# Stage 2 of three batches in other product shapes, four low parts on GpSimd, and another slot for the state rows' operand

## The chip, the cores and the metric

The kernel runs on one core of a Trainium2 chip. The metric is the device time of one execution in microseconds; lower is better. The engines named below are PE (TensorE: the matrix products), PEld (its weight loads), DVE (VectorE), ACT (ScalarE), POOL (GpSimd) and SP (the queue that issues most DMAs).

## The reference

There are B = 8 batches, H = 8 heads, S = 512 tokens, 32 state rows and D = 64 values per head. Cut to what matters:

```
scores  = x @ state^T / 8;  a  = softmax(scores)      # tokens look at the state
xread   = a @ state
scores2 = state @ x^T / 8;  a2 = softmax(scores2)     # state rows look at the tokens
sread   = a2 @ x
y   = concat([xread, sread], rows)                     # 544 rows a batch, 8 * 64 = 512 wide
out = ((y @ w1) * (y @ w2)) @ w3 @ w_out               # 512 -> 1024 -> 1024 -> 512
```

The weights arrive as float64, x and state as float32; the output is float32.

## The kernel before

**Products at full precision from float32r parts.** A float32 operand is split into a high part (ACT casts it to float32r, L96) and a low part (DVE subtracts the high part, L97). A product is three float32r products: high by low, high by high, low by high. On PE one such product loads 128 x 128 stationary values (LDWEIGHTS) and lets a moved operand of 512 columns stream through.

**Weights.** `w3 @ w_out` is formed once at the start and kept split as `wo_hi` and `wo_lo` (1024 rows in 8 blocks `ft` of 128, 512 columns). For each batch, state times w1 and w2 gives small matrices `sw_hi`, `sw_lo` (L260 to L282), so that stage 1 can go from the attention weights straight to the hidden layer.

**The stages of a batch b.**

- `stage1(b, ft)`, for ft = 0 to 7: 12 products (L306) into one buffer of two PSUM banks (pool `ps_2`, three buffers in rotation, `two_banks()`), one bank for w1, one for w2. Then `hidden`: ACT copies one half (L290), DVE multiplies it with the other (L291), and `split` makes `g_hi` (ACT, L96) and `g_lo` (DVE, L97), [128 hidden values x 512 tokens] each.
- `stage2(gs, tt)`, for tt = 0 to 3: 24 products (`project`, L316; stationary is a 128-token slice of `g_hi` or `g_lo`, moved are 512 columns of `wo_hi` or `wo_lo`) into one bank (pool `ps_o`, two buffers, `bank()`). ACT copies the bank to a `tmp` tile (L329, `store`), and a DMA writes it out.
- After tt = 0, the side steps for batch b + 1 follow in PE's order: two units of `sw` (into `ps_2`), the scores of both softmaxes (into `ps_2`, L146 in the function `per_head`, moved operand `x_d`), the read of the state rows of batch b (into `ps_o`, L242), and two more units of `sw` (into `ps_2`). The softmax work on DVE and ACT then runs beside tt = 1 to 3. The scores are read from PSUM by a DVE transpose (L186), a DVE maximum (L189) and two ACT exponentials (L196).

PE's and SP's orders are those in which the code is written; a buffer of a pool in rotation is free again when its last reader has ended. Batch 0 is handled apart, mixed with the loading and conversion of the weights. `FORMS` in the change speaks of batches 4, 5 and 6.

**State rows.** After batch 7, `state_rows` takes the 256 gathered rows `sread` through the same layers. Its moved operand `grp_sr` holds high and low part side by side; for each of 64 steps a product of 512 columns (L507) and one of 256 columns (L508) alternate, each with its own weights. Its stage 2 is two more calls of `stage2`.

Of the kernel before, what the change touches and what calls it, by code (L numbers as in the profile page):

```python
# [22 lines left out]
F32 = mybir.dt.float32  # L23
F32R = mybir.dt.float32r
# [3 lines left out]
ALU = mybir.AluOpType  # L28
AX = mybir.AxisListType
P = 128  # L30
# [3 lines left out]
LAST = 5  # L34
PARTS = {0: (640, 1024), 1: (512, 1024)}
WARM = 15

@with_exitstack
def attn_bilinear_kernel(
# [10 lines left out]
    nc = tc.nc  # L50
    B, _, NT, H, D = x_s.shape
    S = NT * P
    NP = H // 2
    NS = st.shape[3]
    KT = H * NS // P
    FT, DO = w34_k.shape[0], out.shape[2]
# [9 lines left out]
    att = ctx.enter_context(tc.tile_pool(name="att", bufs=2))  # L66
# [7 lines left out]
    unused = ps_o.tile([P, NF], F32, name="ps_o")  # L74
    for n in range(WARM):
        nc.tensor.matmul(unused[:, :P], zeros, zeros, start=True, stop=True)
# [7 lines left out]
    wo = {part: const.tile([P, FT, DO], F32R, name=f"wo_{part}") for part in ("hi", "lo")}  # L84
    const.tile([P, 32], F32, name="pad_1")

    def bank():
        return ps_o.tile([P, NF], F32, name="ps_o")

    def two_banks():  # L90
        return ps_2.tile([P, 2, NF], F32, name="ps_2")

    def split(hi, lo, src):

        return (
            nc.scalar.copy(out=hi, in_=src),  # L96
            nc.vector.tensor_tensor(out=lo, in0=src, in1=hi.bitcast(F32), op=ALU.subtract),  # L97
        )


# [49 lines left out]
    def load_x(b):  # L150
        sts[b] = att.tile([P, NP, NS], F32, name="st")
        nc.sync.dma_start(out=sts[b], in_=st[b])
        x_tiles[b] = att.tile([P, NP, S], F32, name="x_d", bufs=1)
        nc.sync.dma_start(out=x_tiles[b], in_=x_d[b])

    def load_tokens(b):
        token_tiles[b] = att.tile([P, NT, H, D], F32, name="x_s", bufs=1)
        nc.sync.dma_start(out=token_tiles[b], in_=x_s[b])
# [15 lines left out]
    def attention_steps(b):  # L174
# [3 lines left out]
        def scores():  # L178
# [41 lines left out]
            nc.vector.transpose(out=flat(at), in_=flat(s1))  # L220
            at_tiles[b] = [att.tile([P, KT, S], F32R, name=f"at_{part}", bufs=1) for part in ("hi", "lo")]
            last = split(*at_tiles[b], at)
            yield

# [38 lines left out]
    def sw_steps(b):  # L263
        sw_tiles.setdefault(b, {})

        def unit(half, i):
            ps = two_banks()
            as_q = ps.rearrange("p k (c f) -> p k c f", c=2)
            per_head(as_q, b, lambda rows, j: w_sb[rows, 2 * half:2 * half + 2, i, j])
            sw_tiles[b][half, i] = sw_pair()  # L270
            split(*sw_tiles[b][half, i], ps)

        return [(lambda half=half, i=i: unit(half, i)) for half in range(HALF) for i in range(2)]

    def sw_quarter(b, quarter, i):
        tiles = sw_tiles.setdefault(b, {})
        half, c = divmod(quarter, 2)
        if c == 0:
            tiles[half, i] = sw_pair()
        ps = two_banks()[:, :, :NQ]  # L280
        per_head(ps, b, lambda rows, j: w_sb[rows, quarter, i, j])
        split(*(t[:, :, c * NQ:(c + 1) * NQ] for t in tiles[half, i]), ps)  # L282


    last_split, stored = [], []

    def hidden(ps, n, g_hi, g_lo):
        a_sb = main.tile([P, NF], F32, name="tmp", bufs=4)
        with tc.high_priority():
            nc.scalar.copy(out=a_sb[:, :n], in_=ps[:, 0, :n])  # L290
            nc.vector.tensor_tensor(out=a_sb[:, :n], in0=a_sb[:, :n], in1=ps[:, 1, :n], op=ALU.mult)  # L291
            last_split[:] = split(g_hi, g_lo, a_sb[:, :n])

    def new_g():
        return [main.tile([P, NF], F32R, name=f"g_{part}", bufs=FT) for part in ("hi", "lo")]

    def stage1(b, ft, gs):
        half, c = divmod(ft * P, NF)
        ps = two_banks()
        hi, lo = at_tiles[b]  # L300
        for i in range(2):
            w_hi, w_lo = sw_tiles[b][half, i]
            k = 0
            for kt in range(KT):
                for w, a in ((w_hi, lo), (w_hi, hi), (w_lo, hi)):
                    nc.tensor.matmul(  # L306
                        ps[:, i], w[:, kt, c:c + P], a[:, kt], start=(k == 0), stop=(k == 3 * KT - 1)
                    )
                    k += 1
        gs.append(new_g())  # L310
        hidden(ps, S, *gs[-1])

    def project(ps, gs, tt, ft):
        g_hi, g_lo = (g[:, tt * P:(tt + 1) * P] for g in gs[ft])
        for k, (g, w) in enumerate(((g_hi, "lo"), (g_hi, "hi"), (g_lo, "hi"))):
            nc.tensor.matmul(  # L316
                ps[:, :DO], g, wo[w][:, ft, :], start=(ft == 0 and k == 0), stop=(ft == FT - 1 and k == 2)
            )

    def stage2(gs, tt, dests):  # L320
        ps = bank()
        for ft in range(FT):
            project(ps, gs, tt, ft)
        store(ps, dests)

    def store(ps, dests):
        o = main.tile([P, NF], F32, name="tmp", bufs=4)[:, :DO]
        with tc.high_priority():
            stored[:] = [nc.scalar.copy(out=o, in_=ps[:, :DO])]  # L329
        for (dest, first, n), queue in zip(dests, cycle((nc.scalar, nc.sync))):  # L330
            queue.dma_start(out=dest, in_=o[first:first + n])

# [2 lines left out]
    def side_steps(b):  # L335


        if b == B:
            return [[reads[b - 1]], [], [], []]
        scores, reads[b], a2 = attention_steps(b)  # L340
        w = sw_steps(b)
        softmax = scores()
        first = partial(islice, softmax, 3)
        if b == 1:
            def rest():

                with tc.issue_after(stored[0].ins):
                    yield from softmax

            return [[first], [reads[0], w[0], w[1]], [], [rest], [w[2], w[3]], []]  # L350

        product = partial(islice, softmax, 1)
        return [[w[0], w[1], product, reads[b - 1], w[2], w[3], lambda: softmax], [], [], []]

    def run(steps):
        for step in steps:
            for _ in step() or ():
                pass

    def batch_stage2(b, gs):  # L360
        side = side_steps(b + 1)
        for tt in range(NT):
            stage2(gs, tt, [(out[b, tt * P:(tt + 1) * P], 0, P)])
            run(side[tt])
        if b + 1 < B:
            load_tokens(b + 1)
        if b + 2 < B:
            load_x(b + 2)


    with tc.tile_pool(name="pro", bufs=2) as pro:
# [43 lines left out]
        gs, acc, early = [], [], range(2)  # L415
# [64 lines left out]
        for tt in range(NT):  # L480
            dests = [(out[0, tt * P:(tt + 1) * P], 0, P)]
# [7 lines left out]
    late = ctx.enter_context(tc.tile_pool(name="late", bufs=1))  # L489


    def state_rows():
        n = B * NS

        sr = late.tile([P, NP, 2, n], F32R, name="grp_sr")
        split(sr[:, :, 1], sr[:, :, 0], sread)
        gs = []
        for ft in range(FT):
            quarter, c = divmod(ft * P, NQ)
            ps = two_banks()  # L500
            for i in range(2):
                wh, wl = (late.tile([P, NP * P], F32R, name=f"grp_z{q}", bufs=3) for q in range(2))
                as_w = lambda t: t.rearrange("p (j f) -> p j f", j=NP)
                split(as_w(wh), as_w(wl), w_sb[:, quarter, i, :, c:c + P])
                for kt in range(NP):
                    ks = slice(kt * P, (kt + 1) * P)
                    nc.tensor.matmul(ps[:, i], wh[:, ks], sr[:, kt], start=(kt == 0), stop=False)  # L507
                    nc.tensor.matmul(ps[:, i, :n], wl[:, ks], sr[:, kt, 1], start=False, stop=(kt == NP - 1))  # L508
            gs.append([g[:, :n] for g in new_g()])
            sums = main.tile([P, 2, n], F32, name="tmp", bufs=4)  # L510
            halves = ps.rearrange("p i (half n) -> p i half n", n=n)
            nc.scalar.copy(out=sums, in_=halves[:, :, 1])
            nc.vector.tensor_tensor(out=sums, in0=sums, in1=halves[:, :, 0], op=ALU.add)
            nc.vector.tensor_tensor(out=sums[:, 0], in0=sums[:, 0], in1=sums[:, 1], op=ALU.mult)
            split(*gs[-1], sums[:, 0])
        for tt in range(n // P):
            stage2(gs, tt, [(out[tt * PER + q, S:], q * NS, NS) for q in range(PER)])


    for b in range(1, B):  # L520
        gs = []
        for ft in range(FT):
            stage1(b, ft, gs)
        batch_stage2(b, gs)
    with tc.issue_after(last_split[0].ins), tc.issue_after(last_split[1].ins):
        state_rows()
# [44 lines left out]
```

## Time and profile before

| | |
|---|---|
| timed executions | median 501.03 us (500.69 to 501.37, 2 runs) |
| profiled execution, first to last instruction (the span) | 498.4 us; some 2.6 us of the timed execution lie around it |
| PE busy | 492.3 us, 99% of the span, 3054 product records |
| DVE busy | 285.7 us, 57% |
| ACT busy | 219.3 us, 44% |
| POOL busy | 0.2 us, four small memsets |
| clock granted to PE | 0.999 of full speed over the span |

A product in the trace overlaps the next, since products are pipelined: its own duration (0.39 us for 512 columns) is longer than the distance from its start to the start of the next. What a product costs is that distance. A "timeline" row gives start and duration in us, engine, line, operation and tiles; a row of "groups" gives busy us and mean ns, then idle time ahead.

### The profile page before, as it was taken

To read this page: it belongs to the slowest core of one execution; us is meant where nothing else is said; L and a number is where in the kernel's file an instruction comes from. 1 tells how busy PE (TensorE), PEld (TensorE's weight loads), DVE (VectorE), ACT (ScalarE), POOL (GpSimd) and SP (SyncE) were. 2 spreads that over 40 slices of the span, in tenths; PEclk is the share of its full clock that TensorE was granted. 3 is DMA by queue.
4 is the path that set the end of the run, shared out by engine and by line. 5 is a ranking of instruction groups with operands and counts; after the bars stand their busy time and mean duration, and the time that the engine had idled before them with its cause. 6 is when DMAs were issued, how large, how long until landed. Compare 5 with 4: busy or idle time off the path is not lost.

```text
span 498.4 us, 7562 instructions
## 1 busy us (share of the span) xinstructions
PE 492.3 (99%) x3054; PEld 362.8 (73%) x3054; DVE 285.7 (57%) x394; ACT 219.3 (44%) x325; POOL 0.2 (0%) x4
## 2 busy tenths in 40 slices
PE   8999999999999999999999999999999999999996
PEld 6444467767867886788678867886788678888885
DVE  5669896772539343934393539354934493530780
ACT  4777884443444244334333434243424342431650
POOL 0000000000000000000000000000000000000000
PEclk9999999999999999999999999999999999999999
DMA  8996962013400350035003500350035003301001
GB/s 343 364 380 237 364 264 33 11 47 80 181 22 19 79 189 23 20 79 188 21 27 76 185 22 27 77 184 22 26 78 183 22 26 78 93 24 49 21 1 42
DMA packets 52323, 52.41 MB, mean 105 GB/s; under 512 B 42304, under 2 KB 43328, under 8 KB 47680
## 3 DMA queue, kind: packets, MB, share of 16 engines
q1 hardware_dynamic: 47488, 43.27, 26.3%
q10 hardware_dynamic: 4800, 8.65, 4.6%
q8 instruction: 24, 0.39, 0.3%
q14 instruction: 11, 0.09, 0.1%
HBM read 38.27 MB, written 8.91 MB: 95 GB/s over the span
## 4 chain that ended last, share of the span: by engine, by line
PE 95%; DVE 2%; ACT 2%; DMA 1%; issue 0%; DVEq 0%
PE ps_o L316 38%; PE ps L306 35%; PE ps L146 7%; PE ps L507 3%; PE ps_o L402 3%; PE ps_o L389 3%; PE ps L389 3%; PE ps L508 2%; PE ps_o L242 1%; DMA raw<-in_w_k_dram 1%; ACT ulps L125 0%; ACT w_sb L117 0%; ACT wo_hi L96 0%; DVE w L133 0%; DVE work L204 0%; DVE wo_lo L97 0%
## 5 line engine op out<-in xcount | busy, mean ns | idle before, releaser
L316 PE MATMUL ps_o<-wo_lo,g_hi 128*128 128x512 f32 x272 | 107.0, 394 | 0.0
L316 PE MATMUL ps_o<-wo_hi,g_hi 128*128 128x512 f32 x272 | 106.0, 390 | 0.0
L316 PE MATMUL ps_o<-wo_hi,g_lo 128*128 128x512 f32 x272 | 105.9, 389 | 0.0
L306 PE MATMUL ps<-at_lo,sw_hi 128*128 128x512 f32 x256 | 100.1, 391 | 0.0
L306 PE MATMUL ps<-at_hi,sw_lo 128*128 128x512 f32 x256 | 99.6, 389 | 0.0
L306 PE MATMUL ps<-at_hi,sw_hi 128*128 128x512 f32 x256 | 99.6, 389 | 0.0
L291 DVE TENSOR_TENSOR tmp<-tmp,ps 128x512 f32<-128x512 f32 x64 | 43.9, 687 | 77.0 <-ACT tmp L290 76.9
L97 DVE TENSOR_TENSOR g_lo<-tmp,g_hi 128x512 fp32r<-128x512 f32 (+1 forms) x72 | 47.5, 661 | 41.7 <-ACT g_hi L96 41.6
L96 ACT CAST g_hi<-tmp 128x512 fp32r<-128x512 f32 (+1 forms) x72 | 43.1, 599 | 53.6 <-DVE tmp L291 48.8
L290 ACT COPY tmp<-ps 128x512 f32<-128x512 f32 x64 | 37.7, 589 | 62.8 <-PE ps L306 52.2
L316 PEld LDWEIGHTS ps_o<-wo_lo,g_hi 128*128 128x128 f32 x272 | 51.0, 188 | 18.0 <-issue 7.5
L316 PEld LDWEIGHTS ps_o<-wo_hi,g_lo 128*128 128x128 f32 x272 | 51.1, 188 | 10.8
L316 PEld LDWEIGHTS ps_o<-wo_hi,g_hi 128*128 128x128 f32 x272 | 51.1, 188 | 10.3
L97 DVE TENSOR_TENSOR sw_lo<-ps,sw_hi 128x1024 fp32r<-128x1024 f32 (+1 forms) x34 | 38.4, 1155 | 32.8 <-ACT sw_hi L96 32.8
L306 PEld LDWEIGHTS ps<-at_lo,sw_hi 128*128 128x128 f32 x256 | 48.1, 188 | 10.9 <-issue 1.1
L306 PEld LDWEIGHTS ps<-at_hi,sw_hi 128*128 128x128 f32 x256 | 48.1, 188 | 10.2 <-issue 0.2
L306 PEld LDWEIGHTS ps<-at_hi,sw_lo 128*128 128x128 f32 x256 | 48.1, 188 | 10.0
L329 ACT COPY tmp<-ps_o 128x512 f32<-128x512 f32 x34 | 19.8, 583 | 76.1 <-PE ps_o L316 76.1
L96 ACT CAST sw_hi<-ps 128x1024 fp32r<-128x1024 f32 (+1 forms) x34 | 31.7, 967 | 14.3 <-PE ps L146 14.2
L146 PE MATMUL ps<-w_sb,st 64*32 64x512 f32 (+1 forms) x544 | 31.6, 572 | 0.0
L402 PE MATMUL ps_o<-w_sb,w 128*128 128x512 f32 x64 | 28.5, 599 | 0.1
L402 PEld LDWEIGHTS ps_o<-w_sb,w 128*128 128x128 f32 x64 | 11.8, 190 | 15.9 <-issue 13.8
(65 smaller groups left out, 417.9 us busy)
## 6 DMA issues: line engine op xcount, KB each, us to landing
raw<-in_w_k_dram SPq DMA_DIRECT2D x8, 1024.0 KB, 6.6
x_d<-in_x_d_dram SPq DMA_DIRECT2D x8, 1024.0 KB, 7.1
raw<-in_w_dram SPq DMA_DIRECT2D x8, 1024.0 KB, 6.3
x_s<-in_x_s_dram SPq DMA_DIRECT2D x8, 1024.0 KB, 5.4
out_dram<-tmp ACTq DMA_DIRECT2D x32, 256.0 KB, 2.0
raw<-in_w3t_dram SPq DMA_DIRECT2D x4, 1024.0 KB, 7.2
a_t<-work SPq DMA_DIRECT2D x96, 32.0 KB, 1.9
sread<-turned SPq DMA_DIRECT2D x128, 4.0 KB, 1.7
```

What stands on the lines that cost most here:

```text
L96: nc.scalar.copy(out=hi, in_=src),
L97: nc.vector.tensor_tensor(out=lo, in0=src, in1=hi.bitcast(F32), op=ALU.subtract),
L146: nc.tensor.matmul(ps[j * NS:(j + 1) * NS, q], sts[b][rows, j], moving(rows, j), start=True, stop=True)
L290: nc.scalar.copy(out=a_sb[:, :n], in_=ps[:, 0, :n])
L291: nc.vector.tensor_tensor(out=a_sb[:, :n], in0=a_sb[:, :n], in1=ps[:, 1, :n], op=ALU.mult)
L306: nc.tensor.matmul(ps[:, i], w[:, kt, c:c + P], a[:, kt], start=(k == 0), stop=(k == 3 * KT - 1))
L316: nc.tensor.matmul(ps[:, :DO], g, wo[w][:, ft, :], start=(ft == 0 and k == 0), stop=(ft == FT - 1 and k == 2))
L329: stored[:] = [nc.scalar.copy(out=o, in_=ps[:, :DO])]
L389: nc.tensor.matmul(w34_ps[i][:, :DO], chunks[k][:, DO + i * P:DO + (i + 1) * P], w_out[k], start=(k == 0), stop=(k == FT - 1),)
L402: nc.tensor.matmul(w34_ps[i][:, :DO], w3s[i][:, k * P:(k + 1) * P], w_out[k], start=(k == 0), stop=(k == FT - 1))
L507: nc.tensor.matmul(ps[:, i], wh[:, ks], sr[:, kt], start=(kt == 0), stop=False)
L508: nc.tensor.matmul(ps[:, i, :n], wl[:, ks], sr[:, kt, 1], start=False, stop=(kt == NP - 1))
```

## The change

- `FORMS = {4: 16, 5: "halves", 6: 4}`: in `batch_stage2`, tt = 1, 2 and 3 of these three batches take another form of stage 2; tt = 0 and the other batches keep theirs.
  - Batch 5, "halves": each product of 512 columns becomes two of 256 columns with the same stationary operand (48 products in place of 24 per tt). The two halves go to two banks of one `two_banks()` buffer of `ps_2`, not to a `ps_o` bank, and `store` copies each half by itself.
  - Batches 4 and 6, "runs": one product of 512 columns as before, but the moved row is read as 16 (batch 4) or 4 (batch 6) values of the first half, then as many of the second, in turn. PSUM then holds the columns in that order, written contiguously, and ACT's copy in `store` puts them back.
- In batch 3, `g_lo` of the odd ft (1, 3, 5, 7) is made on GpSimd in place of DVE.
- The state rows' `sr` lies in the slot of `x_s` (pool `att`) in place of a tile of its own in pool `late`; with that the `grp_z` tiles of `late` move to lower addresses.

The diff, cut to its core:

```
+FORMS = {4: 16, 5: "halves", 6: 4}
...
-    def split(hi, lo, src):
+    def split(hi, lo, src, rest=None):
         return (
             nc.scalar.copy(out=hi, in_=src),
-            nc.vector.tensor_tensor(out=lo, in0=src, in1=hi.bitcast(F32), op=ALU.subtract),
+            (rest or nc.vector).tensor_tensor(out=lo, in0=src, in1=hi.bitcast(F32), op=ALU.subtract),
         )
...
-        hidden(ps, S, *gs[-1])
+        hidden(ps, S, *gs[-1], nc.gpsimd if b == 3 and ft % 2 else None)
...
+    def project_halves(ps, gs, tt, ft):
+        g_hi, g_lo = (g[:, tt * P:(tt + 1) * P] for g in gs[ft])
+        for k, (g, w) in enumerate(((g_hi, "lo"), (g_hi, "hi"), (g_lo, "hi"))):
+            for half in range(2):
+                cols = slice(half * DO // 2, (half + 1) * DO // 2)
+                nc.tensor.matmul(
+                    ps[:, half, cols], g, wo[w][:, ft, cols],
+                    start=(ft == 0 and k == 0), stop=(ft == FT - 1 and k == 2),
+                )
+
+    def project_runs(ps, gs, tt, ft, run):
+        g_hi, g_lo = (g[:, tt * P:(tt + 1) * P] for g in gs[ft])
+        for k, (g, w) in enumerate(((g_hi, "lo"), (g_hi, "hi"), (g_lo, "hi"))):
+            nc.tensor.matmul(
+                ps[:, :DO], g, wo[w][:, ft, :].rearrange("p (h c e) -> p c h e", h=2, e=run),
+                start=(ft == 0 and k == 0), stop=(ft == FT - 1 and k == 2),
+            )
+
-    def stage2(gs, tt, dests):
+    def stage2(gs, tt, dests, form=None):
+        if form == "halves":
+            ps = two_banks()
+            for ft in range(FT):
+                project_halves(ps, gs, tt, ft)
+            store(ps, dests, [(slice(h * DO // 2, (h + 1) * DO // 2), ps[:, h, h * DO // 2:(h + 1) * DO // 2]) for h in range(2)])
+            return
         ps = bank()
...
+            if parts:
+                stored[:] = [nc.scalar.copy(out=o[:, cols], in_=src) for cols, src in parts]
+            elif run:
+                stored[:] = [nc.scalar.copy(
+                    out=o.rearrange("p (h c e) -> p c h e", h=2, e=run),
+                    in_=ps[:, :DO].rearrange("p (c h e) -> p c h e", h=2, e=run),
+                )]
...
-            stage2(gs, tt, [(out[b, tt * P:(tt + 1) * P], 0, P)])
+            stage2(gs, tt, [(out[b, tt * P:(tt + 1) * P], 0, P)], FORMS.get(b) if tt else None)
...
-        sr = late.tile([P, NP, 2, n], F32R, name="grp_sr")
+        sr = att.tile([P, NP, 2, n], F32R, name="x_s", bufs=1)
```

How instructions stand before on PE in batch 5, from the scores of batch 6 (the tile `ps_2_2887`) to the first products of tt = 1 (numbers tell buffers apart; `waits` names the semaphores of the engines or DMA queues that a row waits for):

```order
L146 MATMUL ps_2_2887<-x_d_2671,st_2669 32x512 [waits DMAHW3_49]
L146 MATMUL ps_2_2887<-x_d_2671,st_2669 32x512 x7
L242 MATMUL ps_o_2896<-x_s_2667,a2_t_2566 32x64 [waits DMAHW7_49,DMAHW1_49,DMAHW0_49]
L242 MATMUL ps_o_2896<-x_s_2667,a2_t_2566 32x64 [waits DMAHW6_49,DMAHW7_49,DMAHW5_49,DMAHW4_49]
L242 MATMUL ps_o_2896<-x_s_2667,a2_t_2566 32x64 [waits DMAHW4_49,DMAHW0_49]
L242 MATMUL ps_o_2896<-x_s_2667,a2_t_2566 32x64 [waits DMAHW6_49,DMAHW7_49,DMAHW5_49,DMAHW0_49]
L242 MATMUL ps_o_2896<-x_s_2667,a2_t_2566 32x64 x28
L146 MATMUL ps_2_2949<-w_sb_90,st_2669 32x512 [waits DVE_49]
L146 MATMUL ps_2_2949<-w_sb_90,st_2669 32x512 x7
L146 MATMUL ps_2_2962<-w_sb_90,st_2669 32x512 [waits DVE_49]
L146 MATMUL ps_2_2962<-w_sb_90,st_2669 32x512 x7
L316 MATMUL ps_o_3020<-wo_lo_94,g_hi_2686 128x512 [waits Activation_49]
```

The same place on PE in the change, from the last `sw` unit of the side steps (L147 is the old L146, L326 is in `project_halves`):

```order
L147 MATMUL ps_2_2962<-w_sb_90,st_2669 32x512 x7
L326 MATMUL ps_2_3020<-wo_lo_94,g_hi_2686 128x256 [waits DVE_49,PE_49,Activation_49]
L326 MATMUL ps_2_3020<-wo_lo_94,g_hi_2686 128x256
L326 MATMUL ps_2_3020<-wo_hi_93,g_hi_2686 128x256 x2
L326 MATMUL ps_2_3020<-wo_hi_93,g_lo_2687 128x256 x2
L326 MATMUL ps_2_3020<-wo_lo_94,g_hi_2706 128x256 x2
```

The first product of tt = 1 now writes the third `ps_2` buffer after the scores (2949 and 2962 lie between), which is the scores' own place in the rotation of three, and so it waits for readers of `ps_2_2887` on DVE and ACT; before, it waited for a `ps_o` bank. On ACT this is the order there, before (`e2_2980` is what the exponentials of the scores write):

```order
L96 CAST sw_hi_2958<-ps_2_2949 128x1024 [waits PE_49]
L196 ACTIVATE e2_2980,sum2_2981<-ps_2_2887,m2_2977 128x512 [waits DVE_49]
L196 ACTIVATE e2_2980,sum2_2981<-ps_2_2887,m2_2977 128x512
L96 CAST sw_hi_2971<-ps_2_2962 128x1024 [waits PE_49]
L207 ACTIVATE work_2975<-work_2975 128x1024 [waits DMAHW3_49,DMAHW7_49,DMAHW0_49,DVE_49]
L329 COPY tmp_3045<-ps_o_3020 128x512 [waits PE_49]
```

In the change the five rows ahead of the copy stand as before, and two copies of 128 x 256 from `ps_2_3020` take the place of the last.

In batch 3, the last products of tt = 0 on PE before (ft = 6 and 7):

```order
L316 MATMUL ps_o_1959<-wo_lo_94,g_hi_1932 128x512 [waits Activation_49]
L316 MATMUL ps_o_1959<-wo_hi_93,g_hi_1932 128x512
L316 MATMUL ps_o_1959<-wo_hi_93,g_lo_1933 128x512 [waits DVE_49]
L316 MATMUL ps_o_1959<-wo_lo_94,g_hi_1952 128x512 [waits Activation_49]
L316 MATMUL ps_o_1959<-wo_hi_93,g_hi_1952 128x512
L316 MATMUL ps_o_1959<-wo_hi_93,g_lo_1953 128x512 [waits DVE_49]
```

and in the change:

```order
L317 MATMUL ps_o_1959<-wo_lo_94,g_hi_1932 128x512 [waits Activation_49]
L317 MATMUL ps_o_1959<-wo_hi_93,g_hi_1932 128x512
L317 MATMUL ps_o_1959<-wo_hi_93,g_lo_1933 128x512 [waits DVE_49]
L317 MATMUL ps_o_1959<-wo_lo_94,g_hi_1952 128x512 [waits Activation_49]
L317 MATMUL ps_o_1959<-wo_hi_93,g_hi_1952 128x512
L317 MATMUL ps_o_1959<-wo_hi_93,g_lo_1953 128x512 [waits Pool_49]
```

The very last product of tt = 0 there now waits for GpSimd's `g_lo` in place of DVE's. SP's order is unchanged.

More of the change, by code (lines that the diff above doesn't have):

```diff
@@ L285, in attn_bilinear_kernel, with hidden @@
     last_split, stored = [], []
-    def hidden(ps, n, g_hi, g_lo):
+    def hidden(ps, n, g_hi, g_lo, rest=None):
         a_sb = main.tile([P, NF], F32, name="tmp", bufs=4)
@@ L291, in hidden @@
             nc.vector.tensor_tensor(out=a_sb[:, :n], in0=a_sb[:, :n], in1=ps[:, 1, :n], op=ALU.mult)
-            last_split[:] = split(g_hi, g_lo, a_sb[:, :n])
+            last_split[:] = split(g_hi, g_lo, a_sb[:, :n], rest)
     def new_g():
@@ L318, in project, with store @@
             )
-    def stage2(gs, tt, dests):
+    def project_halves(ps, gs, tt, ft):
[21 more added lines that the diff above has]
+            return
         ps = bank()
         for ft in range(FT):
-            project(ps, gs, tt, ft)
-        store(ps, dests)
-    def store(ps, dests):
+            if form:
+                project_runs(ps, gs, tt, ft, form)
+            else:
+                project(ps, gs, tt, ft)
+        store(ps, dests, run=form)
+    def store(ps, dests, parts=None, run=None):
         o = main.tile([P, NF], F32, name="tmp", bufs=4)[:, :DO]
         with tc.high_priority():
-            stored[:] = [nc.scalar.copy(out=o, in_=ps[:, :DO])]
+            if parts:
[5 more added lines that the diff above has]
+                )]
+            else:
+                stored[:] = [nc.scalar.copy(out=o, in_=ps[:, :DO])]
         for (dest, first, n), queue in zip(dests, cycle((nc.scalar, nc.sync))):
```

## The prediction

> **What bounds the kernel now.** I read the page first, then the chain that ended last, then the timeline around the places that the change touches.
>
> ```profile
> span 498.4 us, 7562 instructions
> PE 492.3 (99%) x3054; PEld 362.8 (73%) x3054; DVE 285.7 (57%) x394; ACT 219.3 (44%) x325; POOL 0.2 (0%) x4
> PE 95%; DVE 2%; ACT 2%; DMA 1%; issue 0%; DVEq 0%
> L316 PE MATMUL ps_o<-wo_lo,g_hi 128*128 128x512 f32 x272 | 107.0, 394 | 0.0
> ```
>
> PE is busy for 99% of the span, and 95% of the chain that ended last is PE. The idle column of the stage 2 group is 0.0: no product of it waits. So the time is the sum of what PE is given. A change helps only by shortening PE's stream, and any wait it puts on PE is added in full, since nothing later gives it back.
>
> What a product of 512 columns costs is seen in the timeline of batch 3, tt = 0 (24 products, first and last, behind the end of stage 1):
>
> ```profile
> 239.50 0.39 PE L306 MATMUL ps<-at_hi,sw_hi 128*128 128x512 f32 x1
> 239.72 0.39 PE L306 MATMUL ps<-at_hi,sw_lo 128*128 128x512 f32 x1
> 239.95 0.39 PE L316 MATMUL ps_o<-wo_lo,g_hi 128*128 128x512 f32 x1
> ...
> 245.16 0.39 PE L316 MATMUL ps_o<-wo_hi,g_lo 128*128 128x512 f32 x1
> ```
>
> 23 distances in 5.21 us: 0.227 us each. The stage 1 products ahead (L306), with other operands at other addresses, stand just as far apart. This is the unit of all that follows. A tt of stage 2 is 24 x 0.227 = 5.4 us.
>
> **Part 1: batch 5, where the halves wait.** The first product of tt = 1 needs the PSUM buffer of the next batch's scores, since the rotation of three comes back to it. Before, it needed a `ps_o` bank. The timeline of before, at that point:
>
> ```profile
> 348.88 1.24 DVE L186 STREAM_TRANSPOSE work<-ps 128x1024 f32<-128x1024 f32 x1
> 350.04 0.50 PE L316 MATMUL ps_o<-wo_lo,g_hi 128*128 128x512 f32 x1
> 350.22 1.21 DVE L189 TENSOR_REDUCE m<-ps 128x2 f32<-128x1024 f32 x1
> 351.56 0.13 DVE L190 TENSOR_SCALAR m<-m 128x2 f32<-128x2 f32 x1
> 351.72 0.69 ACT L196 ACTIVATE e<-ps,m 128x512 f32<-128x512 f32 x1 [1.38 <-DVE m L190]
> 352.40 0.68 ACT L196 ACTIVATE e<-ps,m 128x512 f32<-128x512 f32 x1
> 352.98 0.20 ACT L196 ACTIVATION_READ_ACCUMULATOR e<-ps,m 128x1 f32 x1
> ```
>
> PE starts tt = 1 at 350.04. The readers of the scores are the transpose, the maximum and two exponentials; the last, with its accumulator, ends at 352.98 + 0.20 = 353.18. None of them waits for PE between 350.04 and 353.18 (the exponential's idle time was ended by DVE), so they do not move. From DVE's end at 351.69 to ACT's start at 351.72 a release takes 0.03 us; with that PE starts at 353.21. **The new wait is 353.21 - 350.04 = 3.2 us.** If the buffer were released by the end of the exponential itself, at 353.08, it would be 3.1. What is queued behind the waiting product on PE is everything else, so all of it is added. ACT's copies of tt = 1, the `at_hi` cast behind them and stage 1 of batch 6 move along with PE by the same 3.2 us and so add nothing. The second and third tt need the buffers of the last two `sw` units, read last by these:
>
> ```profile
> 352.72 1.22 DVE L97 TENSOR_TENSOR sw_lo<-ps,sw_hi 128x1024 fp32r<-128x1024 f32 x1
> ...
> 354.99 1.22 DVE L97 TENSOR_TENSOR sw_lo<-ps,sw_hi 128x1024 fp32r<-128x1024 f32 x1
> ```
>
> They end by 356.2, and the second tt starts at about 353.2 + 5.4 = 358.6. No wait there.
>
> **Part 2: the price of halves.** 3 tt of 24 products give 72 pairs of 256 columns in place of 72 products of 512, each half with a weight load of its own. The only float32r products of 256 columns in the trace are those of the state rows, where they alternate with products of 512:
>
> ```profile
> L507 PE MATMUL ps<-grp_sr,grp_z 128*128 128x512 f32 x64 | 22.6, 399 | 0.0
> L508 PE MATMUL ps<-grp_sr,grp_z 128*128 128x256 f32 x64 | 18.0, 281 | 0.0
> ...
> 460.73 0.39 PE L507 MATMUL ps<-grp_sr,grp_z 128*128 128x512 f32 x1
> ...
> 461.42 0.40 PE L507 MATMUL ps<-grp_sr,grp_z 128*128 128x512 f32 x1
> 461.66 0.28 PE L508 MATMUL ps<-grp_sr,grp_z 128*128 128x256 f32 x1
> 461.78 0.40 PE L507 MATMUL ps<-grp_sr,grp_z 128*128 128x512 f32 x1
> ...
> 483.33 0.40 PE L316 MATMUL ps_o<-wo_lo,g_hi 128*128 128x512 f32 x1
> ```
>
> 64 steps take 483.33 - 460.73 = 22.60 us, 0.353 us for 768 columns. The low end: a half costs half of 0.227, and nothing is added. The high end: the 512-column product costs 0.227 there too, so the other costs 0.126, a pair 0.252, and 72 x 0.025 = 1.8 us are added. The weight loads cannot be saved: the page counts 3054 loads for 3054 products although neighbours share a stationary operand. Nothing in the rows is nearer to one end, so I take the middle: **+0.9 us.** ACT's additional copies fall into its idle time (44% busy).
>
> **Part 3: the runs.** Batches 4 and 6 keep 72 products of 512 columns each; only the order in which the moved row is read differs. No row here shows a float32r operand read in short runs. The nearest rows that stream 512 columns at another pace are plain float32 products, two records each:
>
> ```profile
> 30.53 1.88 PE L389 MATMUL ps<-w_sb 128*128 128x512 f32 x4
> 32.25 1.88 PE L389 MATMUL ps_o<-w_sb 128*128 128x512 f32 x4
> ```
>
> 4 records in 1.72 us: 0.430 each. The upper end is that the runs slow a product to this pace: 72 x (0.430 - 0.227) = +14.6 us per batch. The lower end is half of a record, 0.215, if the runs take away whatever makes 0.227 of it: 72 x -0.012 = -0.9 us per batch. I take 0, near the lower end, because a run of four float32 values is still a contiguous, aligned piece, and the two halves lie at a fixed distance. ACT's copy reads PSUM in order and writes in runs; in order it takes 0.59 us:
>
> ```profile
> 245.65 0.59 ACT L329 COPY tmp<-ps_o 128x512 f32<-128x512 f32 x1 [3.47 <-PE ps_o L316]
> ```
>
> It had idled for 3.47 us before, and a bank is wanted again only after a whole tt of 5.4 us, so even several times that stays covered.
>
> **Part 4: GpSimd.** Four subtractions leave DVE. DVE is no bound, so nothing is gained. The last one, ft = 7, is wanted soonest. In the trace DVE's starts here:
>
> ```profile
> 242.20 0.69 DVE L97 TENSOR_TENSOR g_lo<-tmp,g_hi 128x512 fp32r<-128x512 f32 x1 [0.69 <-ACT g_hi L96]
> ```
>
> and its reader is the last product of tt = 0 at 245.16 (quoted above). GpSimd has 2.96 us of cover. POOL shows only memsets, so the price is bounded from the same operation on DVE, 0.69 us, and, far above, from DVE's longest row quoted here, 1.24 us on twice the columns, doubled once more: 2.5 us. Both are under 2.96: **0.** Earlier ones have 5.4 us each. If GpSimd took more, PE would wait for the rest.
>
> The Trainium skill (GPSIMD Engine Reference, section 3.1) gives a GpSimd tensor_tensor add 1.96 times DVE's time; by that, 1.35 us as an estimate, and the sum would not change. POOL's rows here cannot show it.
>
> **Part 5: the slot.** The state rows' split waits for the same gathered rows as before, and `x_s` is read last in the side steps of batch 7, far ahead. Only addresses change. The 64 steps cost 0.353 against 0.227 + 0.113 = 0.340 if both products ran at the common pace: at best -0.8 us, and +0.4 at the other end, if all were like the longer step from 461.42 to 461.78, 0.36. Stage 1 and stage 2 keep one pace with operands at different addresses, so I take 0.
>
> **Sum.** 3.2 + 0.9 + 0 + 0 + 0 = +4.1 us on the profiled 498.4: a span of 502.5. The timed median lies 2.6 us above the span; 501.03 + 4.1 = **505.1 us**, 0.8% more.
>
> **The rivals.**
>
> *The clock falls in the wait* (to 507.1). PE stands idle for about 3.1 us in the middle of the run, which it does nowhere now. At the end of the trace:
>
> ```profile
> 494.01 0.39 PE L316 MATMUL ps_o<-wo_hi,g_lo 128*128 128x512 f32 x1
> ...
> 493.90:497.30 3.40, 0.50 (x3) 0.08 (x1) 0.00 (x0) 0.59 (x1) 0.00 (x0) 1.00 0.29 77
> 497.30:498.40 1.10, 0.00 (x0) 0.00 (x0) 0.00 (x0) 0.00 (x0) 0.00 (x0) 0.51 0.00 0
> ```
>
> PE ends at 494.40; the granted clock (third column from the end) is 1.00 up to 497.30 and 0.51 after it. So 2.9 us of idling were enough there. The price comes from the start of the kernel, where PE is cold:
>
> ```profile
> 1.04 5.87 PE L76 MATMUL ps_o<-work 128*128 128x128 f32 x30 [1.04 <-DVE work L73]
> ```
>
> 30 records of 128 columns at a quarter of 0.430 would be 3.2 us; they took 5.9. A cold start costs up to 2.6 us, and here only a window's remainder: I take 2.0, so 505.1 + 2.0 = 507.1. Against it: one such fall says nothing about where in the observation the idle time must lie.
>
> The Trainium skill (TensorE: Matmul & The Clock Gate, "Part 1: The HAM clock gate") has the gate judge free-running windows of about 3.4 us and close after an idle one. By that rule an idle time just under a window closes the gate only in part of all positions, which speaks against the full price in every run; the trace's 2.9 us at the end agrees that less than a whole window can do.
>
> *Short reads are costly* (slower by over 2%). If reading runs of four in batch 6 halves the pace as for plain float32, 505.1 + 14.6 = 519.7; both batches give 534.3. It decides from the point where the two batches together add 5.9 us more (511.05 is 2% above 501.03), 41 ns for each of 144 products. For it: nothing here shows such a read. Against it: nothing in the rows shows a pace that depends on which addresses a product reads.
>
> *The wait is not there* (not slower than can be told). If the halves found a free buffer, or the exponentials ran earlier, the 3.2 us fall away: 501.03 + 0.9 = 501.9, and with halves at their low end 501.0. This decides only if the last reader ended by 350.04; the rows put it 3.1 us later, so little speaks for it.
>
> *GpSimd is late* (to 507). At 5 us in place of 0.69, PE would wait 2 us in batch 3.
>
> **How the numbers follow.** Wait and halves as forecast, clock held: 0.43. The clock falls: 0.32. Costly short reads: 0.10. No wait: 0.08. Late GpSimd: 0.07. The range takes in the first two with the ends of the unknown costs: down to 501.03 + 3.2 - 0.9 - 0.8 = 502.5, up to 501.03 + 3.2 + 1.8 + 0.4 + 2.0 = 508.4. Two per cent is about what a measurement of this kernel can tell from no change: slower by more needs the costly short reads, 0.10; faster by more, 10 us off PE's stream, has no term here, 0.01; within it 0.89.
>
> **What the profile of the changed kernel would show.** A PE idle time of 3.2 us ahead of the first 256-column product in batch 5, ended by ACT's exponential; distances of 0.113 to 0.126 us between halves; 0.227 us for the runs of both lengths; POOL's subtractions under 3 us and no PE wait for them; state row steps at 0.353; a granted clock of 1.00 right behind the wait, or 0.5 for some us if the first rival holds. I am wrong if PE does not wait in batch 5, or if the alternating reads move away from 0.227 by more than some ns.

## The result and the profile after

The changed kernel takes 508.23 us (508.10 to 508.35, 2 runs) against 501.03: the ratio is 1.0144, with an interval of 1.0115 to 1.0174. The forecast was 505.1; the measured time lies inside the predicted range of 502.5 to 508.4, 0.2 below its upper end. The profiled execution went from a span of 498.4 us to 506.6, 8.2 more.

The head of the page and two of its rows by slices, of the changed kernel:

```profile
span 506.6 us, 7718 instructions
PE 497.2 (98%) x3126; PEld 367.9 (73%) x3126; DVE 283.1 (56%) x390; ACT 219.9 (43%) x328; POOL 5.4 (1%) x8
PEclk9999999999999999999999999999899999999999
PE 93%; DVE 3%; ACT 2%; DMA 1%; issue 0%; DVEq 0%; ACTq 0%
```

PE has 72 more products (3126) and is still the bound, but its clock row, all 9 before, now holds an 8, and DVE has 3% of the chain where it had 2%. The timeline at tt = 1 of batch 5 (L326 is a half, x2 means two of them):

```profile
353.36 0.68 ACT L197 ACTIVATE e<-ps,m 128x512 f32<-128x512 f32 x1
353.93 0.20 ACT L197 ACTIVATION_READ_ACCUMULATOR e<-ps,m 128x1 f32 x1
354.19 0.80 PE L326 MATMUL ps<-wo_lo,g_hi 128*128 128x256 f32 x2 [3.11 <-ACT e L197]
354.78 0.63 PE L326 MATMUL ps<-wo_hi,g_hi 128*128 128x256 f32 x2
355.21 0.63 PE L326 MATMUL ps<-wo_hi,g_lo 128*128 128x256 f32 x2
...
357.28 0.40 PE L326 MATMUL ps<-wo_hi,g_hi 128*128 128x256 f32 x2
357.51 0.40 PE L326 MATMUL ps<-wo_hi,g_lo 128*128 128x256 f32 x2
357.75 0.40 PE L326 MATMUL ps<-wo_lo,g_hi 128*128 128x256 f32 x2
```

PE idles for 3.11 us until the second exponential has ended: the wait that was forecast, at its place and with its releaser. Behind it, pairs of halves stand 0.43 us apart at first and 0.24 us from 357.28 on. The reason is in the stretches (window and length, busy us of PE, PEld, DVE, ACT and POOL with their instruction counts, granted clock, then DMA share and GB/s):

```profile
350.00:353.70 3.70, 1.07 (x24) 0.16 (x16) 3.70 (x7) 2.03 (x4) 0.00 (x0) 1.00 0.00 0
353.80:357.10 3.30, 2.92 (x13) 2.92 (x14) 3.30 (x4) 2.26 (x4) 0.00 (x0) 0.50 0.05 7
357.20:360.50 3.30, 3.30 (x29) 3.30 (x29) 3.20 (x7) 0.00 (x0) 0.00 (x0) 1.00 0.04 5
```

The clock is 0.50 in the middle stretch: the first rival held as well. From 354.19 to 357.28 there are 14 halves in 3.09 us; at 0.120 us they would have taken 1.68, so about 1.4 us are lost, 0.1 of it the usual late first product. The halves at full clock, and the runs of 16 (batch 4) and 4 (batch 6):

```profile
371.91 0.40 PE L326 MATMUL ps<-wo_hi,g_lo 128*128 128x256 f32 x2
...
372.87 0.40 PE L307 MATMUL ps<-at_lo,sw_hi 128*128 128x512 f32 x1
```

```profile
306.01 0.40 PE L334 MATMUL ps_o<-wo_hi,g_hi 128*128 128x512 f32 x1
...
307.93 0.40 PE L334 MATMUL ps_o<-wo_lo,g_hi 128*128 128x512 f32 x1
```

```profile
422.73 0.42 PE L334 MATMUL ps_o<-wo_hi,g_hi 128*128 128x512 f32 x1
...
423.98 0.40 PE L307 MATMUL ps<-at_lo,sw_hi 128*128 128x512 f32 x1
```

8 halves in 0.96 us are 0.120 each. 8 products in runs of 16 take 1.92 us, 0.240 each; 5 in runs of 4 take 1.25, 0.250 each. The plain one is 0.227 as before. GpSimd and the state rows, as groups:

```profile
L98 POOL TENSOR_TENSOR g_lo<-tmp,g_hi 128x512 fp32r<-128x512 f32 x4 | 5.2, 1290 | 237.9 <-ACT g_hi L97 237.9
L543 PE MATMUL ps<-x_s,grp_z 128*128 128x512 f32 x64 | 22.6, 399 | 0.0
L544 PE MATMUL ps<-x_s,grp_z 128*128 128x256 f32 x64 | 18.0, 281 | 0.0
```

GpSimd takes 1.29 us and PE waits for none of its four results; the state rows' groups read as before to the last digit. The account of the 8.2 us: wait 3.2 (the first product of tt = 1 moved from 350.04 to 354.19, of which 0.96 is the 72 runs of batch 4 ahead of it; 3.11 is idling), clock 1.3, halves 72 x (0.240 - 0.227) = 0.9, runs 72 x 0.013 + 72 x 0.023 = 2.6, together 8.0.

### The profile page after: what moved, and what is told of

Its sections match the earlier page's. It is cut to its first block, busy times and chain, and to the rows that moved or that the text cites. A ratio compares the mean times of both kernels' runs of the same rounds, so it can differ in the third digit from the quotient of the medians.

```text
span 506.6 us, 7718 instructions
## 1 busy us (share of the span) xinstructions
PE 497.2 (98%) x3126; PEld 367.9 (73%) x3126; DVE 283.1 (56%) x390; ACT 219.9 (43%) x328; POOL 5.4 (1%) x8
## 4 chain that ended last, share of the span: by engine, by line
PE 93%; DVE 3%; ACT 2%; DMA 1%; issue 0%; DVEq 0%; ACTq 0%
PE ps L307 34%; PE ps_o L317 27%; PE ps_o L334 7%; PE ps L147 7%; PE ps L326 4%; PE ps L543 3%; PE ps_o L438 3%; PE ps_o L425 3%; PE ps L425 3%; PE ps L544 1%; PE ps_o L243 1%; DMA raw<-in_w_k_dram 1%; DVE work L187 0%; DVE m L190 0%; ACT ulps L126 0%; ACT w_sb L118 0%
## 5 line engine op out<-in xcount | busy, mean ns | idle before, releaser
L317 PE MATMUL ps_o<-wo_lo,g_hi 128*128 128x512 f32 x200 | 78.7, 393 | 0.0
L317 PE MATMUL ps_o<-wo_hi,g_hi 128*128 128x512 f32 x200 | 77.9, 390 | 0.0
L317 PE MATMUL ps_o<-wo_hi,g_lo 128*128 128x512 f32 x200 | 77.9, 389 | 0.0
L98 DVE TENSOR_TENSOR g_lo<-tmp,g_hi 128x512 fp32r<-128x512 f32 (+1 forms) x68 | 44.8, 660 | 38.8 <-ACT g_hi L97 38.7
L317 PEld LDWEIGHTS ps_o<-wo_lo,g_hi 128*128 128x128 f32 x200 | 37.5, 188 | 12.8 <-issue 5.0
L317 PEld LDWEIGHTS ps_o<-wo_hi,g_lo 128*128 128x128 f32 x200 | 37.5, 188 | 8.0 <-DVE g_lo L98 0.2
L317 PEld LDWEIGHTS ps_o<-wo_hi,g_hi 128*128 128x128 f32 x200 | 37.5, 188 | 7.5
L365 ACT COPY tmp<-ps_o 128x512 f32<-128x512 f32 x25 | 14.6, 583 | 62.4 <-PE ps_o L317 62.4
L147 PE MATMUL ps<-w_sb,st 64*32 64x512 f32 (+1 forms) x544 | 31.6, 572 | 0.0
L438 PEld LDWEIGHTS ps_o<-w_sb,w 128*128 128x128 f32 x64 | 11.8, 190 | 15.9 <-issue 14.6
```

The source lines that it names most:

```text
L98: (rest or nc.vector).tensor_tensor(out=lo, in0=src, in1=hi.bitcast(F32), op=ALU.subtract),
L147: nc.tensor.matmul(ps[j * NS:(j + 1) * NS, q], sts[b][rows, j], moving(rows, j), start=True, stop=True)
L317: nc.tensor.matmul(ps[:, :DO], g, wo[w][:, ft, :], start=(ft == 0 and k == 0), stop=(ft == FT - 1 and k == 2))
L438: nc.tensor.matmul(w34_ps[i][:, :DO], w3s[i][:, k * P:(k + 1) * P], w_out[k], start=(k == 0), stop=(k == FT - 1))
```

## The experiments

**1. Halves from tt = 2 on.**

```
-            stage2(gs, tt, [...], FORMS.get(b) if tt else None)
+            stage2(gs, tt, [...], FORMS.get(b) if tt > (b == 5) else None)
```

> The changed kernel, but in batch 5 the halves begin with tt = 2; tt = 1 keeps products of 512 columns into a ps_o bank. The buffer of the scores is then wanted 5.4 us later, after its last reader has ended. Theory (the wait for the scores' buffer costs 3.2 us, the clock that falls in it 1.2, a pair of halves 13 ns more than one product): no PE idle time, clock 1.00 throughout, and 3.2 + 1.2 + 24 x 0.013 = 4.7 us off, 508.2 to 503.5. Rival (the first halves of a batch are dear by themselves, whatever they wait for): the first products of tt = 2 are as dear as those of tt = 1 were, and only 0.3 us go.

Measured: 504.17 us against 500.92 for the kernel before on the same chip, ratio 1.0063 (1.0048 to 1.0079). The first halves, in the timeline of this kernel:

```profile
356.35 0.39 PE L317 MATMUL ps_o<-wo_hi,g_lo 128*128 128x512 f32 x1
356.58 0.40 PE L326 MATMUL ps<-wo_lo,g_hi 128*128 128x256 f32 x2
356.81 0.40 PE L326 MATMUL ps<-wo_hi,g_hi 128*128 128x256 f32 x2
```

No idle time, and 0.24 a pair from the first one on. What is left above the kernel before, 3.2 us, is what runs (2.6) and 48 pairs of halves (0.6) cost. It is the wait, with the clock that fell in it, and not the form that was dear.

**2. The wait filled with products.**

```
         if form == "halves":
+            if tt == 1:
+                filler = bank()
+                for n in range(13):
+                    nc.tensor.matmul(filler[:, :DO], gs[0][0][:, :P], wo["hi"][:, 0, :], start=True, stop=True)
             ps = two_banks()
```

> The changed kernel with 13 additional products of 512 columns (2.95 us, into a ps_o bank that nobody reads) ahead of the halves of tt = 1 in batch 5: PE works through most of the wait. Theory (the clock fell because PE stood idle): the clock stays at 1.00, the halves start at the same time as in the changed kernel and run at 0.120 us from the first, and 1.2 us go, 508.2 to 507.0. Rival (the first 13 halves ran at 0.213 us because of work beside them on DVE and ACT): they stay at 0.213 us and the time stays at 508.2.

Measured: 507.53 us against 500.92, ratio 1.0129 (1.0113 to 1.0145). In this kernel's timeline and stretches:

```profile
351.45 3.24 PE L344 MATMUL ps_o<-wo_hi,g_hi 128*128 128x512 f32 x13
354.63 0.50 PE L326 MATMUL ps<-wo_lo,g_hi 128*128 128x256 f32 x2
354.97 0.39 PE L326 MATMUL ps<-wo_hi,g_hi 128*128 128x256 f32 x2
355.20 0.40 PE L326 MATMUL ps<-wo_hi,g_lo 128*128 128x256 f32 x2
```

```profile
354.60:358.00 3.40, 3.40 (x29) 3.37 (x29) 3.40 (x5) 1.94 (x2) 0.00 (x0) 1.00 0.06 10
```

The halves still start 3.18 us after PE came free at 351.45, but the clock stays at 1.00 and they run at 0.24 a pair, with DVE busy throughout in both and ACT for 1.94 of 3.40 us against 2.26 of 3.30. So the slow first halves were the clock's doing. In the trace the 144 halves take 17.24 us from first start to last, in the changed kernel 18.57: the clock costs 1.3 us. The timed runs agree in direction, 6.6 above before against 7.2, but they are not on record for the same chip, and 0.6 us is within what the kernel before scatters.

**3. The runs alone.** The kernel before with `FORMS = {4: 16, 6: 4}`.

> The kernel before with the runs in batches 4 (16) and 6 (4) alone; no halves, GpSimd and slot as before. Theory (a product read in runs of 16 takes 0.240 us, in runs of 4 0.250, in place of 0.227): 72 x 0.0133 + 72 x 0.0235 = +2.6 us, 501.0 to 503.6. Rival (the longer distances came from where the clock and the wait put these products in time, or from GpSimd's neighbours): 0.227 and no change.

Measured: 503.44 us against 500.92, ratio 1.0046 (1.0031 to 1.0062), +2.5 us. The distances in its trace are 0.240 us for nearly every product of batch 4 and 0.246 and 0.254 in turn in batch 6. The cost belongs to the reading order alone.

**4. GpSimd and the slot alone.** The changed kernel with `FORMS = {}`.

> The changed kernel without any other form of stage 2: only GpSimd's four low parts in batch 3 and the state rows' operand in the slot of x_s. Theory (both are covered): no change, 501.0, GpSimd 1.3 us each, state rows at 0.353 us a step. Rival (the part of the difference that the trace does not explain is theirs): up to 0.5 us either way.

Measured: 500.90 us against 500.92, ratio 1.0001 (0.9991 to 1.0010). Both parts cost nothing.

**5. Half the filling**, 6 products in place of 13 in experiment 2.

> As with 13 additional products ahead of the first halves of batch 5, but 6 (1.4 us): PE idles 1.8 us instead of 3.1. Theory that the clock falls only when most of a stretch of 3.4 us is idle: the clock stays at 1.00 and the halves run at 0.120 us from the first. Rival (any idle time over about a microsecond lets it fall): 0.5 for about 3.4 us, and the first halves at 0.213.

Measured: 507.82 us against 500.54, ratio 1.0137 (1.0109 to 1.0165). The stretch of idling and the one after it:

```profile
353.30:354.80 1.50, 0.02 (x1) 0.00 (x0) 1.50 (x3) 1.46 (x5) 0.00 (x0) 1.00 0.02 3
354.80:358.20 3.40, 3.36 (x28) 3.36 (x29) 3.40 (x5) 1.95 (x2) 0.00 (x0) 1.00 0.06 10
```

PE idles for 1.5 us and the clock stays. An idle time of half the length is harmless in this execution; experiment 7 says more on that.

**6. Other orders of reading, and fewer weights.** The kernel before with a form of its own for each tt, cut to its core:

```
+FORMS = {1: [(2, 2), (2, 8), (2, 32)], 2: [(2, 64), (2, 128), (4, 16)], ...,
+         5: [(8, 4), (64, 4), (2, 1)], 6: ["narrow", "narrow", None], ...}
+                ps[:, :DO], g, wo[w][:, ft, :].rearrange("p (h c e) -> p c h e", h=run[0], e=run[1]),
...
+        if form == "narrow":
...
+                g_hi, g_lo = (g[:, tt * P:tt * P + P // 2] for g in gs[ft])
...
+                        ps[:P // 2, :DO], g, wo[w][:, ft, :], ...
```

> The kernel before, with every tt = 1 to 3 of batches 1 to 7 in a form of its own: runs of e values from each of h pieces of the moved row in turn (the change has h = 2 with e = 16 and 4). Two tiles (batch 6, tt = 1 and 2) load only 64 stationary columns, leave out the other 64 tokens and store the first 64 twice. Theory that jumps cost (each change of run costs something): 0.227 for runs of 128, rising with the number of jumps, the same for every h at one e; at e = 16 always 0.240. Rival that the distance of the jump costs (two places of a row that get in each other's way): at e = 16 the value changes with h, from 1024 bytes (h = 2) to 128 bytes (h = 16). Second rival, that only runs shorter than four values cost much (a line is read more than once): 0.25 at e = 4 or more, 0.4 or more at e = 2 and 1. For the 64 columns: if the 0.014 us that a product takes above 512 columns at full clock (0.213) are reads of the weights, 0.220; if they are fixed for each product, 0.227.

Measured, in us from start to start (mean over the products of a tile from the fifth on; an estimate to compare with: in the changed kernel five pairs of halves, 512 columns each, took 356.91 - 354.78 = 2.13 us at half clock, which at full clock would be 0.213 a pair):

| h pieces, e values | us | | h, e | us |
|---|---|---|---|---|
| plain | 0.227 | | 4, 64 | 0.227 |
| 2, 128 | 0.227 | | 4, 32 | 0.233 |
| 2, 64 | 0.228 | | 4, 16 | 0.231 |
| 2, 32 | 0.237 | | 4, 4 | 0.268 |
| 2, 16 | 0.240 | | 8, 32 | 0.237 |
| 2, 8 | 0.243 | | 8, 16 | 0.239 |
| 2, 4 | 0.250 | | 8, 4 | 0.276 |
| 2, 2 | 0.333 | | 16, 16 | 0.240 |
| **2, 1** | **0.216** | | 32, 4 / 64, 4 | 0.223 / 0.231 |

With 64 stationary columns, in two tiles that leave out half of their tokens, a product takes 0.230. None of the three theories fits: the cost rises with the number of jumps from e = 128 down to 2, but at one e it also changes with h (e = 4: 0.223 to 0.276), and with single values of two halves it vanishes. The weights theory falls too: half the weights do not shorten a product. How far a product lies above the 0.213, from 0.003 us to 0.120, goes with the order in which the moved row is read. Differences of 0.004 are not to be read: the form 32, 4 took 0.227 when experiment 8 repeated it. The last two tiles of batch 5, at the change from 64, 4 to 2, 1:

```profile
368.29 0.39 PE L338 MATMUL ps_o<-wo_hi,g_lo 128*128 128x512 f32 x1
368.52 0.38 PE L338 MATMUL ps_o<-wo_lo,g_hi 128*128 128x512 f32 x1
368.74 0.38 PE L338 MATMUL ps_o<-wo_hi,g_hi 128*128 128x512 f32 x1
...
373.49 0.38 PE L338 MATMUL ps_o<-wo_hi,g_lo 128*128 128x512 f32 x1
373.70 0.40 PE L311 MATMUL ps<-at_lo,sw_hi 128*128 128x512 f32 x1
```

24 products in 373.70 - 368.52 = 5.18 us, 0.216 each.

**7. The changed kernel again.** Nothing edited.

> The changed kernel once more, in more rounds. Theory (wait 3.2, clock 1.3, halves 1.0, runs 2.5): 508 in nearly all executions if the clock falls in each, or two groups about 1.3 us apart if it falls only in some, with the mean clock of the run 0.003 lower where it falls. Rival (the clock plays no part in the time): one group, whatever the clock.

Measured: 508.96 us (508.44 to 510.37, 5 runs) against 500.54, ratio 1.0165 (1.0143 to 1.0188). The mean clocks of the five were 0.995 in three executions (508.87 to 509.27), 1.000 in the fastest (508.44) and 0.992 in the longest (510.37). So the clock does not fall alike in each. A fall for 3.4 us takes 0.0034 off the mean (0.5 x 3.4 of 507 us), and the kernel before, whose clock falls only behind its last product, never reads under 0.998. So the four under 0.998 had such a fall in the wait, and of the two executions in the section on the result the one at 508.10, with 0.998, had none: in all, the clock fell in five of seven. That the time follows the clock is not shown by these times: no two groups 1.3 us apart stand out, the execution without a fall lies 0.4 to 0.8 below the three, and the kernel before scatters from 500.15 to 502.49 at clocks of 0.999 and 1.000. The profiled spans on this chip do agree, 507.2 here against 505.9 in experiment 5, where the clock held; the 144 halves took 18.75 us here and 17.25 there. The profiled one shows when it fell:

```profile
351.40:354.50 3.10, 0.03 (x4) 0.00 (x0) 3.10 (x7) 1.72 (x6) 0.00 (x0) 1.00 0.01 1
354.55:355.60 1.05, 1.05 (x8) 1.05 (x9) 1.05 (x2) 0.85 (x1) 0.00 (x0) 1.00 0.06 8
355.70:359.00 3.30, 3.30 (x18) 3.30 (x17) 3.27 (x7) 1.06 (x1) 0.00 (x0) 0.50 0.06 10
```

PE had idled until 354.55 and worked again for 1.1 us before the clock fell. A judgement of a stretch of time, not of the moment, fits that. The Trainium skill (TensorE: Matmul & The Clock Gate, Part 1) has free-running windows of about 3.4 us; the trace agrees with the length, 0.50 holds for 3.4 us (353.8 to 357.2 and 355.7 to 359.1), but a window with a third of work in it was enough here, so it need not be idle.

The clock records in all eleven traces bear this out. In each, the clock stays at 1.00 for a whole number of times 3.413 us before it falls (144 in the kernel before, 102 in the changed one, 103 here), wherever PE's work begins and ends. Cut into such stretches from the clock's first rise on, the traces show this ahead of a fall and where it held:

| trace | stretch of 3.41 us from | PE busy in it, us | clock behind it |
|---|---|---|---|
| before, at the end | 493.90 | 0.50 | 0.5 |
| changed | 350.36 | 0.71 | 0.5 |
| experiment 6, at the end | 501.36 | 0.91 | 0.5 |
| experiment 7 | 352.26 | 1.12 | 0.5 |
| changed, at the end | 500.55 | 1.90 | 1.0 |
| experiment 9 | 446.60 | 1.92 | 1.0 |
| experiment 5 | 350.93 | 2.39 | 1.0 |

No stretch with 1.12 us of work or less kept the clock, and none with 1.90 or more lost it; nothing lies between. As an estimate from these rows, an idle time of 3.1 us leaves at least one stretch with 0.3 to 1.9 us of work, depending on where the stretches happen to lie, so whether the clock falls is a matter of position. An idle time of 1.5 us leaves at least 1.9, which no trace shows to be too little.

**8. More orders**, as in experiment 6, with e = 1 and 2 for other h.

```
+FORMS = {1: [(4, 1), (8, 1), (16, 1)], 2: [(32, 1), (64, 1), (128, 1)], 3: [(256, 1), (4, 2), (16, 2)],
+         4: [(64, 2), (16, 4), (32, 8)], 5: [(128, 2), (16, 8), (2, 1)], 6: [(32, 4), (32, 2), None],
+         7: [(64, 8), (8, 2), (2, 1)]}
```

> The kernel before, again with tt = 1 to 3 of batches 1 to 7 in forms of their own (batch 6, tt = 3 keeps the plain one), chosen after single values of two halves in turn (h = 2, e = 1) had taken 0.216 us and pairs (h = 2, e = 2) 0.333. Theory P (each pair of reads that follow each other must come from two places; single values do that, pairs and longer runs only at their ends): e = 1 gives 0.216 for every h from 4 to 256 and e = 2 about 0.333 for every h. Rival D (it is the distance of 1024 bytes alone): h = 4 and above with e = 1 is 0.227 or more, and h = 256, which reads every second value, has its own pace.

Measured, one run, 568.38 us. With e = 1: h = 2 again 0.216 (twice), h = 4 0.283, h = 8 0.487, h = 16 to 256 between 0.431 and 0.461. With e = 2: h = 4 0.443, h = 8 0.487, other h 0.431 to 0.462. The longer runs of this kernel took 0.246 (16, 4), 0.227 (32, 4), 0.230 (16, 8), 0.232 (32, 8) and 0.227 (64, 8). Two neighbours of h = 4, e = 1:

```profile
154.75 0.45 PE L338 MATMUL ps_o<-wo_lo,g_hi 128*128 128x512 f32 x1
155.03 0.45 PE L338 MATMUL ps_o<-wo_hi,g_hi 128*128 128x512 f32 x1
```

Theory P falls: single values are good only at h = 2, that is 1024 bytes apart. For single values rival D is what is left, as a description and not as a mechanism; pairs at the same 1024 bytes cost 0.333, so the distance alone does not make a form good. It also shows that the feared rival of the prediction, a product at twice the time, exists, though for shorter runs than those of the change.

**9. All float32r products with paired reads.** The kernel before; the splits write `at`, `wo` and `sr` in an order that comes out right when read in pairs.

```
+    def paired(t):
+        return t.rearrange("p (h c) -> p c h", h=2)
+    def split_paired(hi, lo, src):
+        dims = "p k" if len(src.shape) == 3 else "p"
+        halves = lambda t: t.rearrange(f"{dims} (h c) -> {dims} h c", h=2)
+        return split(halves(hi), halves(lo), src.rearrange(f"{dims} (c h) -> {dims} h c", h=2))
...
-                        ps[:, i], w[:, kt, c:c + P], a[:, kt], start=(k == 0), stop=(k == 3 * KT - 1)
+                        ps[:, i], w[:, kt, c:c + P], paired(a[:, kt]), start=(k == 0), stop=(k == 3 * KT - 1)
...
-                ps[:, :DO], g, wo[w][:, ft, :], start=...
+                ps[:, :DO], g, paired(wo[w][:, ft, :]), start=...
```

> The kernel before, with every float32r product of stage 1, stage 2 and the state rows reading its moved row as single values of its two halves in turn; the splits write at, wo and sr in the order that gives the natural one when so read, so nothing is put back later. Theory (the 0.216 us of h = 2, e = 1 belongs to this order of reading and not to the tile of batch 5): 768 products of stage 1 and 816 of stage 2 save 0.011 us each, 17.4 us, and the state rows some 1.5: 500.9 to about 482. The splits read with a step of two values, 28 longer rows at most beside PE. Rival (0.216 came with the place of that one tile): stage 1 and stage 2 at 0.227 and no change, or some at 0.24 and a longer time.

Measured: 486.42 us (485.65 to 488.33, 4 runs) against 500.79, ratio 0.9723 (0.9695 to 0.9750). This version beats both kernels. Its page and groups:

```profile
span 483.9 us, 7559 instructions
L326 PE MATMUL ps_o<-wo_lo,g_hi 128*128 128x512 f32 x272 | 104.2, 383 | 0.9 <-ACT g_hi L106 0.9
L326 PE MATMUL ps_o<-wo_hi,g_lo 128*128 128x512 f32 x272 | 103.2, 379 | 0.5 <-DVE g_lo L107 0.5
L106 ACT CAST at_hi<-work 128x1024 fp32r<-128x1024 f32 x8 | 12.1, 1508 | 27.0 <-DVE work L230 27.0
```

The typical distance in its trace is 0.216 us in stage 1 and stage 2 alike, and the state rows take 0.219 and 0.109. Some 4.5 us of the expected 19 did not come. For 3.9 of them PE idles where it did not before: 0.9 us for ACT's and 0.5 for DVE's part of g in the rows above, and elsewhere in its trace 1.0 us in batch 0 and 1.5 ahead of the state rows. The casts of `at`, which read with a step of two values, take 1508 ns where they took 1050. The Trainium skill (TensorE: Matmul & The Clock Gate, Part 1) puts 512 columns, in its measurements of bf16, at 215.7 ns; by the measured 0.216 us float32r reaches that pace in this reading order, alone among those tried here.

## Why the prediction was right, and where not

- **The wait** (Part 1): 3.2 us forecast, 3.11 of idling and 3.2 from start to start measured, released by the second exponential. The buffer rotation and four rows of the timeline gave it whole. Experiment 1 took it away.
- **The halves** (Part 2): +0.9 forecast as the middle of 0 to 1.8, measured 0.120 us each, 0.9. The middle was taken because "Nothing in the rows is nearer to one end", and that was a misreading: its own rows at 461.66 and 461.78 put 0.12 us behind a 256-column product, a pair at 0.24, and 0.24 behind the 512-column one at 461.42, where the high end assumed 0.227. The number came out right by luck, though the rows would have given it.
- **The runs** (Part 3): 0 forecast, 2.6 measured, 2.5 by experiment 3 alone. This term was mis-sized. Its bounds of -0.9 to +14.6 a batch held, but "near the lower end, because a run of four float32 values is still a contiguous, aligned piece" was an argument without a row. Runs of 4 cost 0.250 us a product and runs of 16 0.240, and the forecast's own sign of being wrong, reads that "move away from 0.227 by more than some ns", is there: 13 and 23 ns. The lower end, 0.215, exists too, but in an order that the argument did not have in mind (single values, experiment 6).
- **GpSimd and the slot** (Parts 4 and 5): 0 forecast, 0 measured (experiment 4); 1.29 us under a cover of 2.96.
- **The clock** (first rival): given 0.32 at 2.0 us, it fell in both profiled executions of the changed kernel and, by the mean clocks, in five of seven timed ones, for 1.3 us in the first trace and 1.5 in the second. The price was over-sized by taking a cold start for it, the chance under-sized: the 2.9 us at the end of the trace of before were the better witness. That it falls "only in part of all positions" came true, but does not follow from the rule cited for it: 3.1 us of idling fill no whole window of 3.4. What makes it so is that a stretch with some work in it is enough (experiment 7).
- **The number**: 505.1 was for the case with the clock held; with the runs it would have been 505.1 + 2.6 = 507.7, with the clock as well 509.0, and 508.2 and 509.0 were measured. That 508.2 lies in the range is partly luck. The range took in the low end of the runs but nothing of theirs above 0; what room there was came from upper ends that were not used up, 0.9 of the halves, 0.4 of the slot and 0.7 of the clock, 2.0 together against 2.6. The median of two executions, one of them without the fall, lies below 509.0 and so inside; that of experiment 7, 508.96, lies above the range.

## What to carry to other kernels

Where an operand moves to another buffer pool, find who had the buffer before and when its last reader ends; on a kernel that is 98% one engine that wait is paid in full, and a few microseconds of idling on PE can cost its clock on top (here 3.1 us did in most executions, 1.5 us did not). The order in which a moved operand is read is a price of its own, to be measured in a table of forms rather than argued: here it decided between 0.216, 0.227 and 0.487 us for the same product.

## What was not expected of the hardware

A float32r product of 512 columns takes 0.227 us when it reads its row straight, 0.216 when it takes single values of two halves 1024 bytes apart in turn, and 0.333 with pairs of values from the same two halves. Single values from places 512 bytes apart cost 0.283, from 256 bytes apart 0.487. Why, these runs don't show; with half of the stationary columns it took 0.230, so their number is not the reason. The clock fell by half for 3.4 us although PE had already worked again for 1.1 us; it fell behind stretches of 3.41 us with at most 1.12 us of work, and held behind those with 1.90 or more.
